# A decode attention kernel: the last two rows a partition of one output projection are loaded apart, by eight small DMAs

## The chip, the cores and the metric

The kernel runs on one core of one Trainium2 chip. The metric is the device time of one execution in microseconds (us). Times inside an execution are counted from the start of the profiled span, which is mostly 1.7 to 2.0 us shorter than the whole time. A difference of one microsecond is 0.12% here. Every run in this document counts as a fast run. There is one trace for each label: the first execution of a changed kernel is also the profiled one, and for the kernel before it is a run of its own (823.21 us). The calls ran on different chips (e1 to e4, e5 to e8, e9 to e11 and e12 on one chip each), so the sure comparisons are those within a call.

## The reference, cut to what matters

Two independent decode attentions, A and B, with one query row, 32 heads of 128 and a model width of 512. A attends to all 16384 keys of its cache, B to the last 4096.

```python
q = (x @ wq)                                     # 1 x 4096
scores = einsum("bhqd,bhkd->bhqk", q, k) * Dh ** -0.5
o = einsum("bhqk,bhkd->bhqd", softmax(scores), v)
y = o.reshape(1, 1, 4096) @ wo                   # wo: 4096 x 512
return concatenate([yA, yB], axis=-1)            # 1 x 1 x 1024
```

The caches make nearly all of the 352 MB that must be read from memory. The two output projections wo (4 MB each) are the last things loaded.

## The kernel before

Keys stream through two k buffers and values through one v buffer of 64 KB a partition each. After the last unit of values, wo takes the v buffer. Row p*32+j of wo lies on partition p, so a partition holds 32 rows of 1 KB of A and 32 of B.

```python
def _load_wo(nc, cx, st, j0, n):                 # one DMA, all 128 partitions, n rows each
    ...
    src = st.wo.rearrange("(p j) f -> p j f", j=J)
    cx.o(nc.sync.dma_start(out=st.wo_t[:, j0 : j0 + n, :], in_=src[:, j0 : j0 + n, :]))

pieces = [(stA, 0, J // 2), (stA, J // 2, J // 2)]           # J = 32
for x in (J // 2, J // 4, J // 8, J // 16, J // 16):         # B: 16, 8, 4, 2, 2 rows
    pieces.append((stB, j0, x)); j0 += x

# the load queue, in order: ..., k of the last unit, v of the unit before, v of the last unit
# (in a k buffer), then the seven pieces

def _out(nc, cx, st, j0, n):
    if j0 == 0:
        st.oc = ...                              # the head outputs, 128 x 32
        cx.o(nc.vector.tensor_copy(st.oc[:, :], st.oc_ps[:, 0:J]))
    ...
    for j in range(j0, j0 + n):
        for x in range(st.cols):
            cx.o(nc.tensor.matmul(out[x], lhsT=st.oc[:, j : j + 1],
                rhs=st.wo_t[:, j, x * w : (x + 1) * w], start=(j == 0), stop=(j == J - 1)))
    if j0 + n == J:
        ...                                      # copy the row, send it out
```

The softmax here doesn't subtract the row's maximum and nothing guards it: scores larger than these inputs give would overflow.

## Time and profile before

Three executions took 822.95, 822.95 and 823.23 us.

The first fence holds lines of the page of the kernel before: busy time of each engine, the DMA engines' busy tenths in 40 slices, and two DMA queues (packets, MB, share of 16 engines' span).

```profile
PE 301.1 (37%) x2148; PEld 117.3 (14%) x2148; DVE 600.7 (73%) x146; ACT 35.1 (4%) x133; POOL 1.3 (0%) x9
...
DMA  9999999999999999999999999999999999999997
...
q1 hardware_dynamic: 8212, 352.33, 99.3%
q8 instruction: 16, 0.26, 0.1%
```

The DMA engines are busy throughout. The second queue, with 16 packets, brings instructions. The next fence is the end of the chain of waits (start, length, what).

```profile
789.00 29.16 DMA wo_t<-in_B_wo_dram
...
818.21 0.43 PE out_ps L307 x4
818.63 0.41 DVE rowB L316
```

The chain ends on the last piece of B's wo: four matmuls, one copy, and the output leaves. So the end is set by the DMA engine that finishes last, not by the mean of the 16. The issue times come next, from the timeline of the load queue's issuer (start, length, line, what).

```profile
785.35 0.81 SPq L146 DMA_DIRECT2D wo_t<-in_A_wo_dram  x2
786.21 3.12 SPq L146 DMA_DIRECT2D wo_t<-in_B_wo_dram  x5
```

All seven pieces are issued between 785 and 790 us, while the queue still has values to load. So nothing runs dry. The issuer's own waits show one short wait among these issues, for a landing of B's values (us, times, longest):

```profile
SPq L146 <- DMA vt<-in_B_v_cache_dram: 0.9, 1, 0.9
```

At the end PE has time to spare, as the timeline shows (start, busy us, what, and the idle time before it).

```profile
796.44 1.90 PE L231 MATMUL acc<-vt,p_sb 128*16 128x512 bf16 x32 [3.79 <-ACT p_sb L212]
798.69 1.90 PE L231 MATMUL acc<-vt,p_sb 128*16 128x512 bf16 x32 [0.34 <-DMA vt<-in_B_v_cache_dram]
...
803.73 8.75 PE L307 MATMUL out_ps<-wo_t,ocA 128*1 128x512 bf16 x32 [0.25 <-DVE ocA L300]
...
818.21 0.38 PE L307 MATMUL out_ps<-wo_t,ocB 128*1 128x256 bf16 x4 [0.29 <-DMA wo_t<-in_B_wo_dram]
```

A profile line says nothing of single DMA engines, but the trace keeps each packet's start, length and size. In steady state a packet starts 3 to 4 ns before the one ahead of it on its engine is recorded as ended, so the packets can be chained into 16 engines. In the kernel before, eight engines end their last packet at 814.7 to 815.6 us and eight at 817.4 to 817.8 us. The late eight are the chains that hold the instruction packets (the second queue above): each of the 16 packets of 16 KB took 0.88 to 1.00 us and set one engine back by about 1.42 us on average, and they went round the same eight engines twice. (The prediction below quotes these ends on the trace's own clock, 11.54 us ahead of the span's.)

### The profile page before, as it was taken

How to read it: one execution, taken by the hardware profiler on the slowest of the kernel's cores; microseconds unless marked ns; L12 is line 12 of the kernel's file. 1: busy time of each engine (PE TensorE's matmuls, PEld its weight loads, DVE VectorE, ACT ScalarE, POOL GpSimd, SP SyncE). 2: the span in 40 equal slices, each digit the busy share in tenths (PEclk: the TensorE clock that was granted, in tenths of full speed). 3: DMA queues.
4: the chain of work that ended last, by engine and by line, in shares of the span. 5: the costliest groups of instructions: out<-in, count | busy, mean ns of one | idle time of the engine just before them, and what ended most of it. 6: DMA issues, size and time to landing. Idle time of an engine off the chain costs nothing.

```text
span 821.2 us, 4767 instructions
## 1 busy us (share of the span) xinstructions
PE 301.1 (37%) x2148; PEld 117.3 (14%) x2148; DVE 600.7 (73%) x146; ACT 35.1 (4%) x133; POOL 1.3 (0%) x9
## 2 busy tenths in 40 slices
PE   3433705143223415060606151423414250606076
PEld 1111202011011102020202020101101020202033
DVE  2099895997496867799196949599659677689921
ACT  0100000000010000000001000000001000000010
POOL 0000000000000000000000000000000000000000
PEclk9855668586767677675858585857666676768599
DMA  9999999999999999999999999999999999999997
GB/s 383 434 457 412 456 412 454 412 454 418 427 442 444 425 441 429 441 416 447 421 445 437 431 435 434 432 423 443 441 418 451 425 445 421 448 413 455 413 424 317
DMA packets 8235, 352.62 MB, mean 429 GB/s; under 512 B 916, under 2 KB 920, under 8 KB 1304
## 3 DMA queue, kind: packets, MB, share of 16 engines
q1 hardware_dynamic: 8212, 352.33, 99.3%
q8 instruction: 16, 0.26, 0.1%
q14 instruction: 3, 0.02, 0.0%
q10 hardware_dynamic: 4, 0.00, 0.0%
HBM read 352.32 MB, written 0.00 MB: 429 GB/s over the span
## 4 chain that ended last, share of the span: by engine, by line
DMA 61%; issue 15%; DVE 13%; PE 11%; ACT 0%; SPq 0%; DVEq 0%
DMA kt<-in_A_k_cache_dram 42%; DMA vt<-in_A_v_cache_dram 12%; PE red L190 7%; DVE kt L178 6%; DVE kt L169 4%; PE acc L231 4%; DMA vt<-in_B_v_cache_dram 4%; DMA wo_t<-in_B_wo_dram 4%; DVE sc L206 2%; ACT p_sb L212 0%; SPq L115 0%; PE out_ps L307 0%; DVE rowB L316 0%; DVEq L169 0%
## 5 line engine op out<-in xcount | busy, mean ns | idle before, releaser
L169 DVE TENSOR_TENSOR kt<-kt,qallA 128x32768 bf16<-128x32768 bf16 (+2 forms) x20 | 276.2, 13810 | 162.5 <-DMA kt<-in_A_k_cache_dram 162.5
L231 PE MATMUL acc<-vt,p_sb 128*8 128x512 bf16 (+1 forms) x1280 | 113.0, 530 | 444.4 <-ACT p_sb L212 344.4
L178 DVE TENSOR_TENSOR kt<-kt 128x16384 bf16<-128x16384 bf16 (+2 forms) x24 | 174.3, 7261 | 0.2
L190 PE MATMUL red<-kt,ident 128*128 128x512 bf16 x640 | 151.2, 396 | 54.6 <-DVE kt L178 54.6
L231 PEld LDWEIGHTS <-p_sb 128*8 128x8 bf16 (+1 forms) x1280 | 37.6, 112 | 515.7 <-ACT p_sb L212 419.8
L190 PEld LDWEIGHTS <-ident 128*128 128x128 bf16 x640 | 63.0, 101 | 142.2 <-issue 47.1
L169 DVE TENSOR_TENSOR kt<-kt,qallB 128x16384 bf16<-128x16384 bf16 x8 | 69.5, 8686 | 2.9 <-DMA kt<-in_B_k_cache_dram 2.9
L206 DVE TENSOR_REDUCE sc<-red 128x256 f32<-128x2048 f32 x20 | 45.7, 2284 | 5.6 <-PE red L190 5.6
L212 ACT ACTIVATE p_sb<-sc,offA 128x256 bf16<-128x256 f32 x32 | 16.0, 500 | 574.7 <-DVE sc L206 574.7
L245 DVE TENSOR_TENSOR acc<-acc,maskA 128x512 f32<-128x512 f32 x16 | 11.1, 694 | 21.4 <-PE acc L231 21.4
L212 ACT ACTIVATE p_sb<-sc,offB 128x128 bf16<-128x128 f32 x32 | 12.4, 388 | 161.2 <-DVE sc L206 161.2
L130 PE MATMUL q_ps<-wq_t,scr 128*128 128x512 bf16 x64 | 15.7, 407 | 6.9 <-DMA wq_t<-in_A_wq_dram 4.9
L251 DVE TENSOR_REDUCE s<-acc 128x128 f32<-128x512 f32 x24 | 16.6, 691 | 0.8
L307 PE MATMUL out_ps<-wo_t,ocA 128*1 128x512 bf16 x32 | 8.8, 443 | 0.3 <-DVE ocA L300 0.3
L245 DVE TENSOR_TENSOR acc<-acc,maskB 128x512 f32<-128x512 f32 x8 | 5.5, 692 | 4.5 <-PE acc L231 4.5
L130 PEld LDWEIGHTS <-scr 128*128 128x128 bf16 x64 | 6.5, 103 | 15.6 <-issue 8.0
L316 DVE CAST rowA<-out_ps 1x512 bf16<-1x512 f32 x1 | 0.7, 678 | 8.8 <-PE out_ps L307 8.8
L259 PE MATMUL f_ps<-s,selA 128*32 128x128 f32 x32 | 6.5, 285 | 0.0
L212 ACT ACTIVATION_READ_ACCUMULATOR p_sb<-sc,offA 128x1 f32 x32 | 6.0, 187 | 0.0
L212 ACT ACTIVATION_READ_ACCUMULATOR p_sb<-sc,offB 128x1 f32 x32 | 6.0, 186 | 0.0
L307 PE MATMUL out_ps<-wo_t,ocB 128*1 128x256 bf16 x64 | 4.3, 272 | 1.8 <-DMA wo_t<-in_B_wo_dram 0.9
L102 DVE CAST scr<-xT 128x128 bf16<-128x128 f32 (+1 forms) x6 | 2.1, 459 | 3.6 <-PE xT L94 3.5
(43 smaller groups left out, 26.4 us busy)
## 6 DMA issues: line engine op xcount, KB each, us to landing
kt<-in_B_k_cache_dram SPq DMA_DIRECT2D x8, 4096.0 KB, 32.4
vt<-in_B_v_cache_dram SPq DMA_DIRECT2D x8, 4096.0 KB, 23.8
wq_t<-in_A_wq_dram SPq DMA_DIRECT2D x1, 4096.0 KB, 12.2
wq_t<-in_B_wq_dram SPq DMA_DIRECT2D x1, 4096.0 KB
wo_t<-in_A_wo_dram SPq DMA_DIRECT2D x2, 2048.0 KB, 22.6
wo_t<-in_B_wo_dram SPq DMA_DIRECT2D x1, 2048.0 KB, 27.0
wo_t<-in_B_wo_dram SPq DMA_DIRECT2D x1, 1024.0 KB, 29.0
wo_t<-in_B_wo_dram SPq DMA_DIRECT2D x1, 512.0 KB
```

The costliest lines, as they stand in the source:

```text
L102: cx.o(nc.vector.tensor_copy(st.xb[:, :, g, :].rearrange("p c (i r) -> p r c i", r=R)[:, g, :, :], xT[:, :].rearrange("p (c o) -> p c o", ...
L130: cx.o(nc.tensor.matmul(q_ps[:, j, :], lhsT=st.xb[:, c, g, :], rhs=w[:, g, j * (512 // DH) : (j + 1) * (512 // DH), :], start=(g == 0 and ...
L169: cx.o(nc.vector.tensor_tensor(out=k, in0=k, in1=q.rearrange("p (o d) -> p o d", o=1).broadcast_to([P, b - a, DH]), op=ALU.mult,))
L178: cx.o(nc.vector.tensor_tensor(out=k[:, :, 0 : DH // 2], in0=k[:, :, 0 : DH // 2], in1=k[:, :, DH // 2 : DH], op=ALU.add,))
L190: cx.o(nc.tensor.matmul(load.red[:, k : k + n, :], lhsT=cx.ident[:, :], rhs=load.kt[:, k : k + n, b * W : (b + 1) * W], start=(b == 0), st ...
L206: cx.o(nc.vector.tensor_reduce(out=sc[:, :], in_=load.red[:, :, :], axis=AX.X, op=ALU.add))
L212: cx.o(nc.scalar.activation(out=u.p[:, :, g, :], in_=sc[:, u.k0 : u.k0 + n].rearrange("p (t e) -> p t e", e=4), func=ACT.Exp, scale=SCALE, ...
L231: cx.o(nc.tensor.matmul(u.acc[r : r + 4 * R, :], lhsT=u.p[:, t, :, :], rhs=u.load.vt[:, k : k + 4, :], start=(t < 4), stop=(t >= T - 4),))
L245: cx.o(nc.vector.tensor_tensor(out=acc, in0=acc, in1=st.mask[:, :].rearrange("p (x o) -> p x o", o=1).broadcast_to([P, 4, DH]), op=ALU.mult,))
L251: cx.o(nc.vector.tensor_reduce(out=u.s[:, :], in_=acc.rearrange("p x d -> p d x"), axis=AX.X, op=ALU.add,))
L259: cx.o(nc.tensor.matmul(cx.f_ps[st.f_at : st.f_at + 32, 0:DH], lhsT=st.sel[:, at : at + 32], rhs=u.s[:, :], start=(u.i == 0), stop=(u.i == ...
L307: cx.o(nc.tensor.matmul(out[x], lhsT=st.oc[:, j : j + 1], rhs=st.wo_t[:, j, x * w : (x + 1) * w], start=(j == 0), stop=(j == J - 1),))
```

## The change

The intent is to take bytes from late engines and give them to early ones. The last two of A's 32 rows a partition are no longer in the pieces. They are 256 KB, regrouped by head into 32 blocks of 8 KB, and are loaded by eight DMAs of 5 or 3 blocks each, meant to use few engines (they ran on 5 and 3, as the packets of the trace after show). They go to rows 0 to 19 and 32 to 43 of a third k buffer; rows 20 to 31 are zeroed. One more matmul ("spread") brings the head outputs into the same order.

```diff
+def _load_apart(nc, cx, st, part):
+    ...
+    if part == 0:
+        cx.wo_x = cx.kt_pool.tile([P, n, APART, st.DN], BF16, tag="kt", name="wo_x")
+        cx.o(nc.gpsimd.memset(cx.wo_x[0:32], 0.0))
+    src = st.wo.rearrange("(h r j) f -> h r j f", h=H, j=J)
+    h0, to, k = ((0, 0, 5), (20, 32, 3))[part]
+    for a in range(4):
+        cx.o(nc.sync.dma_start(
+            out=cx.wo_x[to + a : to + a + 4 * k - 3 : 4],
+            in_=src[h0 + a : h0 + a + 4 * k - 3 : 4, :, J - APART : J, :],
+        ))
 ... (in _fin_rows, after the output rows of all heads)
+            cx.o(nc.tensor.matmul(moved, lhsT=cx.spread[:, :], rhs=..., start=True, stop=True, ...))
+            cx.o(nc.vector.tensor_copy(st.oc_x[:, :], moved))
 ... (in _out)
+    if st.apart and j0 == 0:
+        todo += [(st.oc_x[0:44, i : i + 1], cx.wo_x[0:44, i // st.apart, i % st.apart, :])
+                 for i in range(DH // J * st.apart)]
 ... (the order of the load queue)
-    pieces = [(stA, 0, J // 2), (stA, J // 2, J // 2)]
+    pieces = [(stA, 0, J // 2), (stA, J // 2, J // 2 - APART)]
     for i, p in enumerate(pieces):
         ld.add(None if i else "vt", lambda p=p: _load_wo(nc, cx, *p))
+        if i < 2:
+            ld.add(None if i else "kt", lambda i=i: _load_apart(nc, cx, stA, i))
```

Also changed: A's output row is summed in a bank of its own, both copies of the head outputs come before the output matmuls, and the two sums of the softmax are one matmul of 64 columns.

More of the change, by code (lines that the diff above doesn't have):

```diff
@@ L17 @@
 W = 8
+APART = 2
 KEYS = 256
@@ L146, in _load_wo @@
     cx.o(nc.sync.dma_start(out=st.wo_t[:, j0 : j0 + n, :], in_=src[:, j0 : j0 + n, :]))
+def _load_apart(nc, cx, st, part):
+    J = st.wo.shape[0] // P
+    H = st.wo.shape[0] // DH
+    n = DH // J
+    if part == 0:
[8 more added lines that the diff above has]
+        ))
 def _load_kv(nc, cx, load, which, tag):
@@ L268, in _fin_rows @@
     H = 32
-    for st in sts:
-        cx.o(nc.tensor.matmul(
-            cx.f_ps[st.f_at : st.f_at + H, DH : DH + 1],
-            lhsT=cx.cs[:, st.f_at : st.f_at + H], rhs=cx.ones_col[:, 0:1],
-            start=False, stop=True, skip_group_check=True,
-        ))
+    cx.o(nc.tensor.matmul(
+        cx.f_ps[0 : 2 * H, DH : DH + 1], lhsT=cx.cs[:, :], rhs=cx.ones_col[:, 0:1],
+        start=False, stop=True, skip_group_check=True,
+    ))
     recip = cx.small.tile([2 * H, 1], F32, tag="recip", name="recip")
@@ L280, in _fin_rows @@
     ))
+    cx.out_ps = cx.red_pool.tile([P, 4, 512], F32, tag="red", name="out_ps")
     for st in sts:
@@ L284, in _fin_rows @@
         h = st.f_at
+        if st.apart:
+            moved = cx.out_ps[0:64, 3, 0 : n * st.apart]
+            cx.o(nc.tensor.matmul(
+                moved, lhsT=cx.spread[:, :],
+                rhs=orow[h : h + H, :].rearrange("p (r j) -> p r j", j=J)[:, :, J - st.apart : J],
+                start=True, stop=True, skip_group_check=True,
+            ))
+            st.oc_x = cx.small.tile([64, n * st.apart], BF16, tag="oc_x", name="oc_x")
+            cx.o(nc.vector.tensor_copy(st.oc_x[:, :], moved))
         for r in range(n):
@@ L293, in _fin_rows @@
             ))
+        st.oc = cx.singles.tile([P, J], BF16, tag=f"oc{st.name}", name=f"oc{st.name}")
+        cx.o(nc.vector.tensor_copy(st.oc[:, :], st.oc_ps[:, 0:J]))
 def _out(nc, cx, st, j0, n):
     J = st.wo.shape[0] // P
-    if j0 == 0:
-        st.oc = cx.singles.tile([P, J], BF16, tag=f"oc{st.name}", name=f"oc{st.name}")
-        cx.o(nc.vector.tensor_copy(st.oc[:, :], st.oc_ps[:, 0:J]))
-    if cx.out_ps is None:
-        cx.out_ps = cx.red_pool.tile([P, 2, 512], F32, tag="red", name="out_ps")
     w = st.DN // st.cols
     out = [cx.out_ps[r : r + 1, b, 0:w] for r, b in st.out_at]
-    for j in range(j0, j0 + n):
+    todo = [(st.oc[:, j : j + 1], st.wo_t[:, j, :]) for j in range(j0, j0 + n)]
+    if st.apart and j0 == 0:
+        todo += [
+            (st.oc_x[0:44, i : i + 1], cx.wo_x[0:44, i // st.apart, i % st.apart, :])
+            for i in range(DH // J * st.apart)
+        ]
+    last = j0 + n == J - st.apart
+    for i, (oc, wo) in enumerate(todo):
         for x in range(st.cols):
             cx.o(nc.tensor.matmul(
-                out[x],
-                lhsT=st.oc[:, j : j + 1],
-                rhs=st.wo_t[:, j, x * w : (x + 1) * w],
-                start=(j == 0),
-                stop=(j == J - 1),
+                out[x], lhsT=oc, rhs=wo[:, x * w : (x + 1) * w],
+                start=(j0 == 0 and i == 0), stop=(last and i == len(todo) - 1),
             ))
-    if j0 + n == J:
+    if last:
         row = cx.accs_pool.tile([1, st.DN], BF16, tag="accs", name=f"row{st.name}")
@@ L373, in problem @@
         st.v_view = v_cache[0, :, sk0 : sk0 + W, :]
-        st.out_at = ((0, 0),) if name == "A" else ((64, 0), (96, 1))
+        st.out_at = ((0, 2),) if name == "A" else ((64, 0), (96, 1))
         st.cols = len(st.out_at)
+        st.apart = APART if name == "A" else 0
         st.f_at = 0 if name == "A" else 32
@@ L444 @@
     )
+    cx.spread = cx.singles.tile([32, 64], BF16, tag="spread", name="spread")
+    nc.vector.memset(cx.spread[:, :], 0.0)
+    nc.vector.tensor_copy(cx.spread[:, 0:20], cx.ident[0:32, 0:20])
+    nc.vector.tensor_copy(cx.spread[:, 32:44], cx.ident[0:32, 20:32])
     cx.cs = cx.singles.tile([P, 64], F32, tag="cs", name="cs")
@@ L485 @@
     stB.oc_ps = cx.acc[1]
-    cx.out_ps = None
     _spread_x(nc, cx, stA, 0, 0)
```

## The prediction

> **What bounds the kernel now.** The transfers. In the 40-slice table the DMA engines are busy 90% or more in every slice but the last; 99.3% of their span belongs to the one load queue. VectorE is busy 73%, PE 37%. The chain of waits ends with 29.2 us of DMA wo of B, four output matmuls (0.43 us) and a 0.41 us copy. So the end is set by the DMA engine that finishes its last wo piece last.
>
> **Uneven engines.** I chained the trace's single DMA packets into 16 engines. A 2 KB packet takes 80 ns, a 16 KB packet 608 ns. At the end the engines stand in two groups: eight finish 0.9 to 1.9 us before the median, eight 0.9 to 1.3 us after it (826.2 to 827.1 against 829.0 to 829.4 us on the trace's own clock). The cause is the instruction queue: its 16 packets of 16 KB each set an engine back about 1.42 us, and they go round eight engines twice, so eight lose 2.8 us and eight nothing. [...]
>
> **What the change does.** It takes 2 KB a partition (16 KB an engine) from all engines and gives these 256 KB to a few. [...] Engine 0 (where the one-row output goes) is in the early group. I assume, from the author's choice, that 1 to 4 are too.
>
> - Engines 5 to 15: about -0.60 us. The late eight end at 828.4 to 828.8.
> - Engines 0 to 2: 32 packets of 2 KB, 2.56 - 0.60 = +1.96 us, ending at 828.2 to 828.8 (829.1 if the slowest early one is among them). Engines 3 and 4: +0.7 us.
> - All meet near 828.8: 0.3 to 0.6 us sooner.
>
> **What else moves.** The spread matmul and copy delay A's output by about 0.15 us; six more A matmuls at 0.21 us add 1.3 us; ocB's copy leaves the gap between A and B (0.87 us before). B's first 32 matmuls end near 815.8 instead of 815.3, the later ones near 817.5, just under the last landing at about 817.6. At most 0.2 us is lost.
> The apart tile needs a k buffer, free when the last score matmuls end (792.3), then a GpSimd memset of 4096 elements: 2 to 3.5 us, estimated from 0.42 us for 384. The load queue's issuer stalls from 785.8 to about 796 and issues A's second half near 798. Early engines run dry near 799.9, late ones near 802.3: a small stall of early engines at worst.
>
> **Prediction.** 822.45 us, range 821.9 to 823.2. Chances: faster by over 2% 0.01, within 2% 0.98, slower 0.01.
>
> **What would show it.** Last pieces ending within about 1 us over most engines; packets of the new DMAs on early engines only; PE's last wait on wo of B ending 0.5 us sooner; A's output ending near 813.9.
>
> **What would make it wrong.** Engines 1 to 4 in the late group (+1 us or more); a seventeenth instruction packet near the end (+1 us); PE ending last instead of the transfer; the issuer's stall reaching late engines; run differences of 0.3 us.

Nothing in the traces numbers the engines. In the prediction and in the expectation of e4, the numbers are my names: 0 to 2 for those taken to carry all eight new DMAs, 3 and 4 for those that carry only the first four, 5 to 7 for three more that DMAs of 8 blocks were taken to use. That k blocks use k engines, always the same ones, and the one-row output's among them, was my assumption before the runs; only the counts, 5, 3 and 8 engines, are shown below. In the kernel before, the packet of A's output row (814.78 us) follows a chain of the early group.

## More of the kernel before

The stretches of the tail show what the DMA engines moved. The columns that matter are the last three: the granted clock of TensorE (PE), the DMA share and GB/s. Packets are counted where they start, so a share can pass 1.

```profile
core 0: us, PE busy (x) PEld busy (x) DVE busy (x) ACT busy (x) POOL busy (x), PEclk, DMA share, GB/s
796.00:800.00 4.00, 3.22 (x60) 1.46 (x64) 1.39 (x2) 1.93 (x11) 0.00 (x0) 1.00 0.94 401
800.00:804.00 4.00, 1.79 (x30) 1.06 (x23) 1.74 (x4) 0.36 (x1) 0.00 (x0) 1.00 1.01 426
804.00:808.00 4.00, 4.00 (x13) 1.29 (x12) 0.00 (x0) 0.00 (x0) 0.00 (x0) 0.59 1.03 442
808.00:812.00 4.00, 4.00 (x20) 1.53 (x19) 0.00 (x0) 0.00 (x0) 0.00 (x0) 0.99 0.97 414
```

## The result, and the profile after

The changed kernel took 824.98 (the profiled execution), 822.56, 822.81 and 822.55 us, median 822.68. The kernel before, with one more execution, has a median of 823.09 (822.95 to 823.50). The ratio is 1.0001, 95% interval 0.9983 to 1.0019: no difference that these runs resolve. A ratio here is the mean time of one kernel's fast runs over that of the other's of the same rounds, so not quite the ratio of the medians quoted.

The medians hide the shape. With the five runs of the first experiment, nine executions fall into two kinds: five at 822.45 to 822.81 and four at 823.80 to 824.98. Their mean is 823.34. The kernel before had no such spread in the same sets (822.83 to 823.89). The spans show the split more clearly: 820.7 to 821.0 us in the five good runs and 822.1 to 823.3 in the four others, against 821.1 to 821.8 in the nine runs of the kernel before in e1's call. It is not quite the changed kernel's alone: in the later calls 2 of 27 runs of the kernel before had spans over 822 (822.4 and 822.6). So the question has two halves: is the small gain of the good runs the balance of the engines, and what takes it back in the others?

The page after:

```profile
PE 306.1 (37%) x2153; PEld 118.6 (14%) x2153; DVE 601.1 (73%) x150; ACT 35.1 (4%) x133; POOL 4.8 (1%) x10
...
q8 instruction: 17, 0.28, 0.1%
```

There is now a seventeenth instruction packet, and GpSimd works 3.5 us more. The chain of waits ends otherwise:

```profile
796.92 6.24 PE acc L249 x59
...
806.58 14.09 PE out_ps L337 x98
820.67 0.41 DVE rowB L343
```

In this execution PE ended last, 14.1 us of output matmuls without a wait for a landing. The issuer, from its timeline:

```profile
785.82 0.33 SPq L147 DMA_DIRECT2D wo_t<-in_A_wo_dram  x1
796.43 3.27 SPq L161 DMA_DIRECT2D wo_x<-in_A_wo_dram  x4
799.74 0.44 SPq L147 DMA_DIRECT2D wo_t<-in_A_wo_dram  x1
800.23 4.72 SPq L161 DMA_DIRECT2D wo_x<-in_A_wo_dram  x4
804.99 3.71 SPq L147 DMA_DIRECT2D wo_t<-in_B_wo_dram  x5
```

Four DMAs of 5 blocks took 3.27 us to issue and four of 3 blocks 4.72 us, where the two 128-partition issues beside them took 0.33 and 0.44. Within the 4.72 and the 3.71 us are two new waits. These are the issuer's waits, the one for the GpSimd memset first:

```profile
SPq L161 <- POOL wo_x L157: 10.2, 1, 10.2
...
SPq L161 <- DMA wo_t<-in_A_wo_dram: 1.7, 1, 1.7
SPq L147 <- DMA wo_t<-in_A_wo_dram: 1.5, 1, 1.5
```

By the start of each single issue in the trace, the wait of 1.7 us stands before the seventh apart DMA, which starts at 803.51 when A's first half has landed, and the wait of 1.5 us before B's fourth piece (807.90). The trace also names the semaphore of each issue: the loads use eight of them in turn, and an issue first waits for the landing of the DMA eight places before it, which used the same one. A's first half (785.82 us) is eight places before the seventh apart DMA (803.51 us): both issues name semaphore 106.

A's second half is issued at 799.7 us instead of 785.7, B's first piece at 805.0 instead of 786.2. By then engines had run dry, and the stretches of the tail show it:

```profile
796.00:800.00 4.00, 3.08 (x32) 1.15 (x36) 0.00 (x0) 2.40 (x14) 0.40 (x1) 0.50 0.93 399
800.00:804.00 4.00, 3.34 (x42) 1.18 (x34) 2.17 (x4) 0.00 (x0) 0.00 (x0) 0.73 0.94 376
804.00:808.00 4.00, 2.43 (x17) 1.09 (x18) 1.21 (x5) 0.36 (x1) 0.00 (x0) 0.70 0.97 397
808.00:812.00 4.00, 4.00 (x11) 1.15 (x9) 0.00 (x0) 0.00 (x0) 0.00 (x0) 0.50 0.99 422
```

Between 800 and 808 us the engines moved 376 and 397 GB/s, where the kernel before moved 426 and 442. Over two times 4 us that is 0.38 MB not moved, which at about 430 GB/s is 0.9 us of all engines.

PE, from the timeline, ran its matmuls on B's last values in 6.21 us, where the kernel before took two times 1.90:

```profile
796.92 6.21 PE L249 MATMUL acc<-vt,p_sb 128*16 128x512 bf16 x64 [3.80 <-ACT p_sb L230]
...
806.58 6.48 PE L337 MATMUL out_ps<-wo_t,ocA 128*1 128x512 bf16 x16 [0.27 <-DVE ocA L321]
```

The clock column says why: 0.50 from 796 to 800 and again from 808 to 812, where it was 1.00 and 0.99 before. (In the trace of the kernel before, A's output matmuls start 0.43 us apart under 0.50 and 0.22 us apart under 1.00.) PE had waited 3.8 us in both kernels. The clock records of both traces hold 1.00 or 0.50, each for a whole multiple of 3.41 us (1 to 16 times, the last record apart). In this run the clock fell to half at 795.4 us, while in the kernel before it stayed full until 804.7.

Chained into engines, the trace shows what the change was made for. All last packets end at 816.6 to 817.5 us, except those of one engine, at 818.77. This is only in part the bytes moved: early engines had also lost time while they ran dry, and e5 below shows the groups close without any bytes moved. The new DMAs ran on 5 and 3 engines: there are 32 more completion packets of 4 bytes (948 against 916 under 512 B), 4 x 5 + 4 x 3. In the kernel before, the 916 are the sum of 16 for each of the 57 large loads and one for each of the four transfers of one row.

The engine that ended last finished A's second half at 807.41 and then stood idle until 808.00, although others had started B's first piece by 806.07. Its next two packets took 844 and 902 ns instead of 611. In the trace of the first experiment two engines idled in the same place, until 807.61 and 808.69, and ended at 818.44 and 819.27, with all others by 817.34.

### The profile page after: what moved, and what is told of

The parts are those of the page before. It is cut to its first block, busy times and chain, and to the rows that moved or that the text cites. A ratio compares the mean times of both kernels' runs of the same rounds, so it can differ in the third digit from the quotient of the medians.

```text
span 823.3 us, 4795 instructions
## 1 busy us (share of the span) xinstructions
PE 306.1 (37%) x2153; PEld 118.6 (14%) x2153; DVE 601.1 (73%) x150; ACT 35.1 (4%) x133; POOL 4.8 (1%) x10
## 4 chain that ended last, share of the span: by engine, by line
DMA 57%; PE 15%; issue 15%; DVE 12%; ACT 1%; SPq 0%; DVEq 0%
DMA kt<-in_A_k_cache_dram 41%; DMA vt<-in_A_v_cache_dram 15%; PE red L208 7%; PE acc L249 6%; DVE kt L196 5%; DVE kt L187 4%; DVE sc L224 2%; PE out_ps L337 2%; ACT p_sb L230 1%; SPq L116 0%; DVE acc L263 0%; DVE s L269 0%; DVE rowB L343 0%; PE f_ps L277 0%; ACT orow L294 0%
## 5 line engine op out<-in xcount | busy, mean ns | idle before, releaser
L249 PE MATMUL acc<-vt,p_sb 128*8 128x512 bf16 (+1 forms) x1280 | 116.6, 544 | 442.7 <-ACT p_sb L230 342.4
L157 POOL MEMSET wo_x<- 32x4096 bf16 x1 | 3.5, 3501 | 790.9 <-PE red L208 790.9
```

The source lines that it names most:

```text
L157: cx.o(nc.gpsimd.memset(cx.wo_x[0:32], 0.0))
L249: cx.o(nc.tensor.matmul(u.acc[r : r + 4 * R, :], lhsT=u.p[:, t, :, :], rhs=u.load.vt[:, k : k + 4, :], start=(t < 4), stop=(t >= T - 4),))
```

## The experiments

The theory to be tested: the good runs gain from the balance of the engines; the others lose because the eight DMAs make the issuer late. Rivals: the gain comes from the rearranged copies and sums; the slow runs are PE's clock; all of it is run noise. Unless said otherwise each had five timed rounds, in calls that shared nine runs of the kernel before (four kernels, four, three, and e12 alone). Each edit is given against the changed kernel.

### e1_again: the changed kernel once more

No edit.

> The changed kernel once more, for its spread. Main theory (the gain is the balance of the 16 DMA engines at the end, and single slow runs are PE at half clock in the tail): median 822.4 to 822.8 us, last wo packets of all engines within about 1 us (16.6 to 17.6 in the last tens, not 14.7 to 17.8), and perhaps one run in four near 825. Rival (run differences only): median 822.9 to 823.3, no run near 825.

Measured: 824.30, 823.80, 822.45, 822.67 and 823.91 us, median 823.80, against 823.08 (822.83 to 823.89) for the kernel before. The balance shows as expected in 14 of 16 engines; the times do not. Slow runs are not one in four but three in five. In the profiled one (824.30) PE was not last: the chain ends on B's wo, on the engine that idled until 808.69. So PE's clock, which decided the 824.98 run, is not needed for a slow run.

### e2_no_move: all of the change but the bytes

```diff
-APART = 2
+APART = 0
-        if i < 2:
+        if i < 2 and APART:
```

> The changed kernel with 0 rows apart: no new DMAs, no spread matmul, but A's row in a bank of its own, both oc copies before the output matmuls and one 64-column sum matmul stay. Main theory (engine balance): no gain, 822.9 to 823.2 us, and the engines end in two groups of eight, about 2.7 us apart, as before. Rival (the earlier copies and the own bank are the gain): 822.4 to 822.7 us.

Measured: 823.04 to 823.47, median 823.28, against 823.08. The engines end in two groups again, 814.9 to 815.8 and 817.8 to 818.1. The rearranged copies, the own bank and the single sum are not the gain.

### e3_all16: the same bytes, spread over all engines

```diff
-    h0, to, k = ((0, 0, 5), (20, 32, 3))[part]
-    for a in range(4): ... blocks of 4 x 2 rows on 5 or 3 partitions
+    h0 = 16 * part
+    for a in range(n):
+        cx.o(nc.sync.dma_start(out=cx.wo_x[h0 : h0 + 16, a, :, :],
+                               in_=src[h0 : h0 + 16, a, J - APART : J, :]))
```

> The same 256 KB apart in eight DMAs of 2 KB packets behind the same halves, with the same memset, but each DMA of 16 blocks, so that all 16 engines share it alike. Main theory: no balance, the two groups stay 2.7 us apart, 822.9 to 823.4 us. Rival (the smaller last pieces or the order of the pieces are the gain, whatever engines carry them): 822.4 to 822.7 us, as the changed kernel.

Measured: 824.91 to 826.22, median 825.34. Both expected ranges were missed by 2 us. No gain showed without choosing engines, but this is no clean control: the second four DMAs took 7.91 us to issue, waits included, B's first piece was issued at 805.4, and only 300 GB/s moved between 804 and 808 us. B's first piece came hardly later than in the changed kernel (805.0), so most of these 2 us came after it; why is not shown.

### e4_k8: eight engines instead of five, no memset

```diff
-        cx.o(nc.gpsimd.memset(cx.wo_x[0:32], 0.0))
-    for a in range(4): ... 5 or 3 blocks, both parts
+    for a in (2 * part, 2 * part + 1):
+        cx.o(nc.sync.dma_start(out=cx.wo_x[a : a + 29 : 4],
+                               in_=src[a : a + 29 : 4, :, J - APART : J, :]))
```

> Four DMAs of 8 blocks on partitions 0 to 31, two behind each half, so no rows to zero and no memset. If engines 0 to 7 are the early group and the issuer's stall (memset 3.5 us, eight DMAs of 0.7 to 1.2 us each) costs time: the second half of A is issued near 794.5 instead of 799.7 and no engine runs dry, all engines end within about 1 us near 816.9, 821.9 to 822.4 us. If engines 5 to 7 belong to the late group: 823.5 us or more, with three engines ending 0.7 us later than before. If the stall costs nothing: 822.5 us.

Measured: 823.32 to 823.71, median 823.45. No engine ran dry (439 GB/s between 804 and 808 us), yet two engines ended last, at 818.27 and 818.32; their chains carry the apart packets. The four DMAs left 32 more completion packets (948 against 916 under 512 B), eight each. The other six late engines ended at 817.0 to 817.3, 0.6 us sooner than before, as predicted for engines that only give bytes away. So among the eight engines that such a DMA uses, two are of the late group. In the changed kernel's trace all carriers stood in the early group before the apart packets began. So 8 blocks reach two late engines, and 5 and 3 don't; 6 or 7 were not tried. The middle expectation failed in size: two engines, not three.

### e5_stall: the stall without the balance

```diff
-APART = 2
+APART = 0
-            out=cx.wo_x[to + a : to + a + 4 * k - 3 : 4], ...
+            out=cx.wo_x[to + a : to + a + 4 * k - 3 : 4, 0:1, 0:1, :], ...   # one row of 1 KB a block
```

The memset and the eight DMAs stay, on the same queue; their 32 KB are read by nothing.

> The stall without the balance: 0 rows apart as in the no-move kernel, but with the memset and the eight DMAs of 5 or 3 blocks on the load queue, each block cut to one row of 1 KB, read by nothing. Theory (the new DMAs make the issuer late, so that B's first wo piece is issued near 805, engines run dry and late engines lose 0.6 to 1.5 us): two groups as before and some engines later still, 823.6 to 825 us. Rival (the late issue costs nothing at the end): 823.1 to 823.4 us, as the no-move kernel.

Measured: 823.49 to 825.07, median 824.35, against 823.04; the interval of the ratio (1.0014, 1.0002 to 1.0027) leaves out 1. The whole time is about 1.1 us above the 823.28 of e2, but part of that lies outside the kernel: three of the five runs spent 2.3 to 2.9 us outside the span. By the spans (821.5 to 822.7, median 822.0, against 821.4 in e2), the stall alone costs about 0.6 us and brings a spread with it. The stretches show the hole:

```profile
800.00:804.00 4.00, 2.43 (x30) 1.16 (x23) 1.84 (x4) 0.03 (x1) 0.00 (x0) 0.92 1.02 411
804.00:808.00 4.00, 3.36 (x17) 1.19 (x17) 0.29 (x2) 0.34 (x1) 0.00 (x0) 0.57 0.91 359
```

One engine ended at 819.40, the other 15 between 816.85 and 817.92. So the two groups, which I had expected to stay, are gone here too, with no bytes moved: early engines that run dry end late. Last packets that end close together are therefore no proof of balance by themselves. What the balance is worth under the same stall isn't resolved either: the best span of e1 (820.7) is 0.8 us under the best one here, but the medians are the same (822.1 and 822.0), and the two calls ran on different chips.

### e6_later: the second four DMAs behind B's first piece

```diff
-        if i < 2:
-            ld.add(None if i else "kt", lambda i=i: _load_apart(nc, cx, stA, i))
+        if i in (0, 2):
+            ld.add(None if i else "kt", lambda i=i: _load_apart(nc, cx, stA, i // 2))
-    if st.apart and j0 == 0:      # apart matmuls in A's first piece
+    if st.apart and last:         # at the end of A's
```

> The changed kernel with the second four DMAs behind B's first piece instead of in front of it, and the apart matmuls at the end of A's. Theory (the issue of B's first piece, held behind eight DMAs and two waits for A's landings, costs the late engines 1.3 to 1.8 us in about half of the runs): B's first piece issued near 800.5 instead of 805, no engine idle at 806 to 808, no run above 823.2, median 822.2 to 822.5 us. Rival (the slow runs are PE's clock): slow runs near 824 stay, as often as before.

Measured: 824.38, 824.55, 823.02, 824.22 and 822.64 us. B's first piece was issued at 799.5, the hole at 804 is gone, and all engines ended by 817.38:

```profile
804.00:808.00 4.00, 3.44 (x24) 1.40 (x24) 0.45 (x3) 0.24 (x1) 0.00 (x0) 1.00 1.02 437
```

But the slow runs stayed, and the chain says why: PE waits for the apart rows, which now land last of A's, and then has 7 us of work left.

```profile
805.12 7.48 DMA wo_x<-in_A_wo_dram
...
812.84 7.14 PE out_ps L337 x53
```

PE was at 0.77 and 0.81 of its clock in these last stretches. So the landings can be mended by the order of the issues, and then PE is the next limit. Neither theory as written was right alone.

### e7_act: the eight DMAs from another queue

```diff
-        cx.o(nc.sync.dma_start(out=cx.wo_x..., 
+        cx.o(nc.scalar.dma_start(out=cx.wo_x...,
+    # part 0 after the last exps, part 1 after the output row; apart matmuls at the end of A's
```

> The eight apart DMAs from ScalarE's queue (four after the last exps, four after the output row), so that the load queue issues all wo pieces at 785 to 789 as before the change. Theory (issuer's stall): no engine runs dry, all packets of the last pieces end by about 817.2, median 821.9 to 822.4 us, no run near 824. Rival (stall costs nothing, the slow runs are PE's clock): 822.5 to 822.7 with some runs near 824.

Measured: 827.64 to 830.18, median 829.24, a clear miss. The load queue was not free at all. It now waited for the other queue's DMAs before B's first piece:

```profile
SPq L147 <- DMA wo_x<-in_A_wo_dram: 23.6, 3, 17.4
```

B's first piece was issued at 803.8, and PE, with late apart rows and a half clock from 815.4 to 822.2, ended at 824.7. In the program as built, the two queues share the eight semaphores: in this trace B's first piece waits on the one that the first apart DMA, from the other queue, had taken at 796.2. In the kernel before, the 0.9 us wait for B's values is of the same kind (two pieces of values and seven of wo are nine DMAs, and the ninth uses the semaphore of the first). No run changed the number of semaphores.

### e8_warm: dummy matmuls in PE's last wait

```diff
+            cx.o(nc.tensor.matmul(stA.oc_ps[:, :], lhsT=cx.ident[:, :], rhs=stA.qall[:, 0:512],
+                start=True, stop=True, skip_group_check=True))       # 16 times, before the last softmax
```

> The changed kernel with 16 dummy matmuls on PE in the wait for the last exps, so that PE's clock stays at full speed into the tail. If the slow runs (two in three above 823.7 in the last set) are PE at half clock: none above 823, median 822.5. If they are the late issue of B's first piece: the slow runs stay, 823.7 to 824.3, only runs like the 824.98 one (PE ending last) go.

Measured: 823.31, 823.15, 824.55, 824.50 and 823.85 us. The clock records of the profiled run have full clock from 785.2 to 822.7 us; one stretch of it:

```profile
804.00:808.00 4.00, 3.61 (x16) 1.26 (x16) 0.17 (x2) 0.00 (x0) 0.00 (x0) 1.00 0.97 392
```

PE ended A's row at 813.3 us, close to the 813.9 of the prediction, and waited for B's landings; one engine, idle from 807.52 to 807.88, ended at 818.28. So slow runs remain with the dummy matmuls in place, which speaks for the issuer. It isn't a clean proof, though: the two slowest runs (824.5) have no trace, and with the 32 more PE instructions of the dummy matmuls the sixteenth instruction packet came at 800.6 us, where it came at 801.3 and 801.7 before.

### e9_short: a memset of half the length

```diff
-        cx.o(nc.gpsimd.memset(cx.wo_x[0:32], 0.0))
+        cx.o(nc.gpsimd.memset(cx.wo_x[0:32].bitcast(F32), 0.0))
```

> The changed kernel with the same memset done as 2048 four-byte elements instead of 4096 two-byte ones: 1.75 us instead of 3.5, so A's second half is issued near 797.5 instead of 799 to 800. Theory (two stalls, the first before A's second half, the second before B's first piece, which waits for two landings of A whatever the memset takes): the engines that ran dry at 800 don't, the dry ones at 806 stay, slow runs stay; median 822.6 to 823.6. Rival (the memset is the whole stall): median 822.2 to 822.5, no run above 823.

Measured: 822.76, 824.06, 822.49, 823.50 and 824.01 us, median 823.50, against 823.27. As the theory has it: the memset took 1.82 us in the chain (3.52 in e1's), A's second half was issued at 796.7 and no engine was dry at 800, but the second four DMAs now took all of the time won, waiting 4.1 us for A's first landing, and B's first piece was issued at 805.0 as before.

```profile
796.72 0.45 SPq L147 DMA_DIRECT2D wo_t<-in_A_wo_dram  x1
797.22 7.75 SPq L161 DMA_DIRECT2D wo_x<-in_A_wo_dram  x4
805.01 3.55 SPq L147 DMA_DIRECT2D wo_t<-in_B_wo_dram  x5
```

That wait is one line of the issuer's waits:

```profile
SPq L161 <- DMA wo_t<-in_A_wo_dram: 4.1, 1, 4.1
```

The seventh apart DMA started at 803.53, as in the changed kernel (803.51), although the issues before it came 3 us sooner.

The slow runs stayed. The profiled run was a good one (822.76), with all engines ending by 817.57. It is the one trace of a good run in this form: all ends within 1 us, PE at full clock from 799.5 us on, and the last packet 0.26 us sooner than in the kernel before.

### e10_late_x and e11_late_x_warm: both stalls and PE's order mended

Second four DMAs behind B's first piece (e6), short memset (e9), and the apart matmuls after those of B's first piece, so that PE need not wait for them; e11 also has the dummy matmuls of e8.

```diff
-    for p in pieces:
+    for p in pieces[:3] + [(stA, J, 0)] + pieces[3:]:    # (stA, J, 0): the apart matmuls
         _out(nc, cx, *p)
```

> Second four DMAs behind B's first piece, short memset, apart matmuls after those of B's first piece. All engines should end by about 817.3. Theory (with the landings mended, PE's clock decides): runs in two kinds, 822.4 to 822.7 where PE is at full clock at the end and 823.5 to 824.5 where it falls to half there. Rival (the landings decide): all 822.3 to 822.7.

> The same with 16 dummy matmuls in PE's wait for the last exps. Theory: PE at full clock to the end in every run, landings by 817.3, median 822.3 to 822.6 with no run above 823, about 0.5 us under the kernel before. Rival (the gain is run noise): 823.0 to 823.3.

Measured, e10: 822.78 to 823.12, median 822.84, against 823.27 (822.99 to 824.30) for the kernel before. No run of the slow kind is left, without any help for the clock, so my expectation of two kinds failed. (Five runs could miss it by chance; with e12 it is none in ten.) e11: 824.09, 823.04, 822.77, 822.82 and 822.78. Its slow run is the profiled one, and the trace shows the risk that the prediction had named: the seventeenth instruction packet came at 817.2 us on an engine with wo packets left, which ended at 818.42, behind the packet's end at 818.20. In e10's profiled run it came at the same time, on an engine that had ended. Whether the dummy matmuls have a part in that is not shown; they bring no gain. In e10 the chain ends on a wait that has nothing to do with loads: B's row waits for A's output transfer to free their common buffer.

```profile
817.56 1.13 DMA out_dram<-rowA
...
818.81 0.42 DVE rowB L343
```

### e12_late_x_row: e10 with a buffer for A's row

```diff
-        row = cx.accs_pool.tile([1, st.DN], BF16, tag="accs", name=f"row{st.name}")
+        pool, tag = (cx.sc_pool, "sc") if st.apart else (cx.accs_pool, "accs")
+        row = pool.tile([1, st.DN], BF16, tag=tag, name=f"row{st.name}")
```

> The late-x kernel again (second four DMAs behind B's first piece, short memset, apart matmuls after those of B's first piece), with A's output row in a buffer of its own, so that B's row copy need not wait for A's output transfer (1.13 us in the last chain of that run). Theory: the wait hid behind PE, which ended only 0.1 us earlier, so 0 to 0.3 us better than the late-x kernel: 822.5 to 822.9 us, no run above 823.2, and 0.3 us or more under the kernel before. Rival (the late-x gain was run noise): 823.0 to 823.3.

Measured: 822.50 to 822.95, median 822.61, against 823.44 (822.99 to 824.11). All five runs are below all nine of the kernel before, and the median span is 820.9 against 821.4. The interval for the ratio (0.9992, 0.9978 to 1.0005) still includes 1, so this is a small gain on the evidence of the samples. Its stretch and chain:

```profile
804.00:808.00 4.00, 3.61 (x25) 1.43 (x25) 0.45 (x3) 0.07 (x1) 0.00 (x0) 1.00 1.05 451
```

```profile
812.69 5.61 PE out_ps L337 x72
818.30 0.41 DVE rowB L344
```

All engines end by 817.31, 0.5 us before the kernel before. Three of them end at 814.5 to 814.7, and eleven at 816.7 to 817.3: with the stall mended, the early engines that carry nothing extra are early again, and the gain is that the last ones end sooner. From 812.7 us on, PE is the limit.

## Why the prediction was right or wrong

- **The time.** 822.68 us measured in the first four runs, 822.45 predicted, inside the range. But the number stands for the good runs only, and that three of the first four runs were good was luck: in e1 two of five were, with a median of 823.80. Over nine runs the mean was 823.34, no gain at all.
- **Bound by the last DMA engine, two groups of eight, instruction packets.** Right for the kernel before, and e2, without the new DMAs, shows the groups again. That the changed kernel closes them is due to the bytes only in part (e5). The six late engines in e4 that only give bytes away end 0.6 us sooner, and e12's last packet 0.5 us: that part is the balance.
- **The new DMAs on early engines only.** Right for 5 and 3 blocks, taken on trust from the choice made in the kernel. e4 shows that the trust was needed: with 8 blocks two carriers were late ones.
- **Ends near 828.8 on the trace's clock, 817.3 on the span's.** Near for 15 of 16 engines (816.6 to 817.5) and wrong for one (818.77). For early engines this was partly chance: by the prediction's own sum (0.60 us less) three of them should have ended near 815 at the latest, and it was the stall that held them up.
- **"The load queue's issuer stalls from 785.8 to about 796 and issues A's second half near 798 ... a small stall of early engines at worst."** This is the step that failed. The memset was right (3.50 us, estimated 2 to 3.5), and early engines did run dry near 799.9. The four issues were mis-sized: the stated times leave about 2 us for them, and they took 3.27, so A's second half came at 799.7. The larger fault is a wait that the sum left out: the seventh apart DMA stood 1.7 us, until 803.5, for A's first half to land, and so B's first piece, which I had given no time, came at 805.0. It was this wait that set it, and neither the memset nor the issue times: in e9 the issues before it came 3 us sooner and B's first piece still at 805.0, and in e3 the first four apart DMAs took 1.75 us and it came at 805.4. Then not only early engines paid: late ones idled too. e5 measured the cost, about 0.6 us of the span, as much as the balance gives (0.5 us in e12). "The issuer's stall reaching late engines" stood in the prediction as a risk.
- **"At most 0.2 us is lost" (on PE).** Right where PE was at full clock in the tail (e8, e9), wrong in the profiled run, where half clock from 795.4 to 802.2 and from 805.6 to 812.4 us made PE last. The prediction says nothing of the clock; its matmul times are those of the one trace before. "PE ending last" stood among its risks.
- **A seventeenth instruction packet.** The pages of the changed kernel, e1 to e6, e9, e10 and e12 count 17, also that of e2, and e11's trace has one at 817.2 us. It was harmless where a trace shows it, but for e11's profiled run: there it cost about 1 us (the span is 822.3 us, that of the other four runs 821.1 or 821.2).

What stays open: why some late engines stood idle after 807.4 us although B's first piece had been issued at 805.0 and others had started it, and why this happens in about half of the executions. No slow run but the profiled ones has a trace. So in the others the seventeenth instruction packet, which cost about 1 us in e11, or PE's clock can't be ruled out.

## What to carry to other kernels

When DMA engines are busy to the end, look at which of them ends last, and ask what else they carried; here small DMAs on 5 and 3 engines brought the last packet 0.5 us forward (e12). Cost such DMAs at the issuer as well as on the engines: here what they held back in the queue cost about as much as they won (0.6 and 0.5 us of the span), and the order of issue decided it. Count, too, how many DMAs may be under way before an issue waits for a landing (eight in this program). When the landings are mended, look at once at what ends last next, here PE and its clock, before more is moved.
